# Gated recurrence and routed experts in one kernel: the turning of each unit's outputs put behind its logits in six units, the matmuls of ones ahead of the work changed from 10 of 512 columns to 40 of 256, and the first unit's state products given another bank

## The chip, the core and the metric

One core of a Trainium2 chip runs the whole program. The metric is the time of one execution on the device in microseconds (us). Of the kernel before there are five timed executions and one that was profiled. Engine names are those of the profile: PE (matmul) and PEld (weight load) are TensorE, DVE is VectorE, ACT is ScalarE, POOL is GpSimd, SP is the engine whose queue issues most DMAs.

## What is computed

```python
# 4 batches x 8 heads, 768 steps, head dim 48
f = 1.0 / (1.0 + np.exp(-f_logit))
for t in range(S):
    state = f[:, :, t, :, None] * state + np.einsum('bhd,bhe->bhde', k[:, :, t], v[:, :, t])
    y[:, :, t] = np.einsum('bhd,bhde->bhe', q[:, :, t], state)
x = y.transpose(0, 2, 1, 3).reshape(3072, 384)
# 4 groups x 4 experts: argmax group, then argmax expert in it, weight g_w * e_w
h = np.maximum(xg[mask_e] @ w1[g, e], 0.0)      # 384 -> 1024
out[tok_idx] = combined[:, None] * (h @ w2[g, e])   # 1024 -> 384
```

## The kernel before, in words

**First stage: the recurrence, in units.** The 768 steps are cut into 6 pieces of 128 (`NC`), the 4 batches into 2 pairs; `units` (L561) lists the 12 units (piece c, pair s), unit i being `(i // 2, i % 2)`. A unit passes through stages, each a Python generator that yields between its parts: `c` (`bounded`, DVE cuts the gate logits off), `g` (`gated`, ACT Exp and Ln, then two running sums over time as matmuls with a triangle, tile cs, L616, and their exponentials, L617 and L618), `m` (`multiplied`, DVE, L636 and L639), `t` (`turned`, 16 transposes of q and k on PE, L650, with four ACT copies, L651), `s` (`scored`, q times k on PE, tile ap, and a mask by DVE, tile am; units 3 to 8 in a halved form, L689 and L692, the others whole, L704 and L707), `n` (`stated`, the products of k and v for the next state, tile ds, L721, and DVE's update of the state, L726 to L729), `w` (`weighed`, the outputs, tile y: the state's part L741, the masks' part L745 or L753; ACT copies them to xT, L756), `d` (`done`, logits lT, L769, an ACT copy L771, and their transposition lg, L774), `x` (`listed`: 8 transposes of the outputs to rows, tile x_ps, L794, and three ACT copies, L796 and L799; these rows are what the experts gather later), `z` (`crossed`, ACT copies, L667), `b` (`decayed`, a transposition of the pieces' decays, tile gt, L659, for which a small DMA, ends, L623, must have landed).

**Order.** PE, DVE, ACT and SP take their instructions in the order in which the program issues them (`manual_schedule`, L85). That order is written out as lists of tokens: `BEGIN` (L844) for the first units, then one list for each i from 3 to 12: `ODD` or `EVEN` (L848, L849), or an entry of `ORDERS`. A token `x-1` in the list of i means: the next part of stage x of unit i-1. `r` advances the routing of a finished piece (`route`, L188): DVE one-hots, a few bf16 matmuls for ranks (tile rk, L213 and L215) and for a table (tile tb, L261, which takes DVE's val, L243), and DMAs of weights and tokens by POOL (L256). `l` issues the loads of a later unit on SP (L591), `o` (L807) writes kept rows to DRAM from SP, `k` (L817) loads the second weights of two early experts, `e` advances these experts.

**PSUM.** Seven banks go round under one tag (`bank`, L80); the eighth belongs to the state products alone: tile ds, allocated once, L534. So every unit's products go to the same place, and the next unit's must wait until DVE has read the last ones.

**Before the first unit** PE multiplies ones with ones (L892 to L894): 10 bf16 matmuls of 512 columns, whose result nobody reads. They wait for nothing but DVE's fill of the ones (L107).

**Second stage: the experts.** Rows are gathered by POOL (xg, L404), turned (L440, or by DVE, L426), multiplied with w1 (hp, L450), rectified by ACT (L451), multiplied with w2 (yo, L471 and L486), scaled, and scattered by POOL (L461). Weights of 1.5 MB each stream in on SP.

Of the kernel before, what the change touches and what calls it, by code (L numbers as in the profile page):

```python
# [10 lines left out]
FP32 = mybir.dt.float32  # L11
# [7 lines left out]
P = 128  # L19
# [4 lines left out]
def kernel(  # L24
# [12 lines left out]
    nc = tc.nc  # L37
    B, H, S, D = q.shape
# [7 lines left out]
    HP = H // 2  # L46
    DP = 64
# [29 lines left out]
    def const(shape, dtype, name):  # L77
        return cp.tile(shape, dtype, tag=name, name=name)

    def bank(shape, name):  # L80
        return ps.tile(shape, FP32, tag="bank", name=name)
# [11 lines left out]
    onesb = const([P, P], BF16, "onesb")  # L93
# [305 lines left out]
    def fetch(pool, rows, n, top=N, late=False):  # L399

        w = {"n": n, "pool": pool, "early": top < N, "late": late, "blocks": [(j, min(P, n - j * P)) for j in range((n + P - 1) // P)]}
        w["x"] = pool.tile([P, len(w["blocks"]), RW], FP32, tag="xg", bufs=2 if pool is ep else 6, name="xg")
        for j, m in w["blocks"]:
            nc.gpsimd.indirect_dma_start(out=w["x"][:, j, :], out_offset=None, in_=x_dram[0:1 + top, :], in_offset=bass.IndirectOffsetOnAxis(ap=rows[:, j:j + 1], axis=0))  # L404
        return w
# [124 lines left out]
    with ExitStack() as fast:  # L530
        sb = fast.enter_context(tc.tile_pool(name="sb", bufs=2))
        fp = fast.enter_context(tc.tile_pool(name="fp", bufs=1))
        sums = fast.enter_context(tc.tile_pool(name="sums", bufs=1, space=bass.MemoryType.PSUM))
        ds = sums.tile([P, 2, HP, D], FP32, tag="ds", name="ds")  # L534

        def kept(shape, name):
            return fp.tile(shape, FP32, tag=name, name=name)
# [24 lines left out]
        NU = len(units)  # L562
# [21 lines left out]
        def load(i, names):  # L584
            c, s = units[i]
            w = live.setdefault(i, {"v": pads["v"][i % 4], "qh": pads["qh"][i % 3]})
            for nm in names:
                if nm not in w:
                    w[nm] = sb.tile([P, 2, H, D], FP32, tag="ld_" + nm, bufs=3 if nm == "f" else 2, name="ld_" + nm)
                for b in parts(i) if nm == "f" else (slice(0, 2),):  # L590
                    nc.sync.dma_start(out=heads(w[nm][:, b])[:, :, 0:D], in_=SRC[nm][2 * s + b.start:2 * s + b.stop, :, c * P:(c + 1) * P, :].rearrange("b h t d -> t (b h) d"))  # L591
# [118 lines left out]
        def stated(i):  # L710

            c, s = units[i]
            w = live[i]
            if c == NC - 1:
                return
            old, new = states[s][c % 2], states[s][(c + 1) % 2]
            wide = D if i else DP
            for a in range(HP):
                for b in range(2):
                    for r in range(2):  # L720
                        nc.tensor.matmul(ds[DP * r:DP * r + wide, b, a, :], lhsT=w["kh"][:, b, 2 * a + r, 0:wide], rhs=w["v"][:, b, 2 * a + r, 0:D], start=True, stop=True)  # L721
            yield
            dst = new[:, :, :, 0:D]
            gv = w["g"].unsqueeze(3).broadcast_to((P, 2, HP, D))
            if c:
                nc.vector.tensor_tensor(dst, old[:, :, :, 0:D], ds, OP.add)  # L726
                nc.vector.tensor_tensor(dst, dst, gv, OP.mult)
            else:
                nc.vector.tensor_tensor(dst, ds, gv, OP.mult)  # L729
            yield  # L730
# [103 lines left out]
        def advance(gens):  # L834
# [6 lines left out]


        STAGES = {"c": bounded, "g": gated, "m": multiplied, "t": turned, "z": crossed, "s": scored, "n": stated, "w": weighed, "d": done, "x": listed, "b": decayed}
        BEGIN = """c0 g0 p g0 g0 m0 m0 m0 m0 l2 t0 t0 t0 t0 h c1 g1 g1 s0 s0 s0 s0 g1 g1 p w0 w0 n0 m1 m1 m1 m1 l3 h x0 x0 x0  # L844
            t1 t1 t1 t1 b1 c2 g2 g2 s1 s1 s1 s1 p d0 g2 g2 n0 n1 w1 w1 m2 m2 l4 n1
            d0 x1 x1 t2 t2 t2 t2 c3 g3 g3 x1 s2 s2 s2 s2 w2 g3 g3 d1 w2 n2 m3 m3 c4 g4 g4""".split()
        BEGUN = 3
        EVEN = "l+2 d-2 n-1 r r r x-1 x-1 t t t t g+1 g+1 x-1 r z s s w s s c+2 d-1 g+2 w g+2 n m+1 m+1".split()  # L848
        ODD = "l+2 d-2 r r x-1 x-1 t t t t b n-1 g+1 g+1 x-1 r z s s w s s c+2 d-1 g+2 w g+2 n m+1 m+1 r n".split()  # L849
        ORDERS = {  # L850
            NU - 4: "l+2 o d-2 n-1 r r r x-1 x-1 t t t t g+1 g+1 x-1 r z s s w s s c+2 d-1 g+2 w g+2 n m+1 m+1".split(),
            NU - 3: "l+2 o d-2 r r x-1 x-1 t t t t b n-1 r g+1 g+1 x-1 r s s s s c+2 w d-1 g+2 w g+2 n m+1 m+1 r n".split(),
            NU - 2: "d-2 r x-1 x-1 r t t t t r g+1 g+1 x-1 s s s s w d-1 w n m+1 m+1 k".split(),
            NU - 1: "d-2 r r n-1 x-1 x-1 t t t t r x-1 r s s s s w b d-1 w r r".split(),
            NU: "d-2 r e d-1 x-1 x-1 d-1 x-1 r r r e e r e r r e r r e r e r r e e e e e".split(),
        }
# [2 lines left out]
        def step(nm, i):  # L859
            if nm == "r":  # L860
                advance(routes)
            elif nm == "e":
                next(first[0], None)
            elif nm == "p":
                next(pad)
            elif nm == "o":
                send_kept(i - (NU - 4))
            elif nm == "k":
                load_second()
            elif nm == "h":  # L870
                next(turning)
            elif 0 <= i < NU:
                if nm == "l":

                    load(i, ("k", "qh"))
                    if i + 1 < NU:
                        load(i + 1, ("f",))
                    load(i, ("v",))
                    return
                if (nm, i) not in steps_of:  # L880
                    steps_of[nm, i] = STAGES[nm](i)
                next(steps_of[nm, i], None)
# [6 lines left out]
        load(1, ("qh", "k"))  # L889
        load(2, ("f",))  # L890
        load(1, ("v",))
        warm = bank([P, 4, P], "warm")  # L892
        for _ in range(10):
            nc.tensor.matmul(warm, lhsT=onesb, rhs=onesb.unsqueeze(1).broadcast_to((P, 4, P)), start=True, stop=True)  # L894
        for tok in BEGIN:
            step(tok[0], int(tok[1:] or 0))
        for i in range(BEGUN, NU + 1):
            if i == BEGUN:
                nc.sync.dma_start(out=x_dram[0:1, 0:DM].rearrange("o (h d) -> o h d", d=D), in_=blank[:, 0:D].unsqueeze(1).broadcast_to((1, H, D)))
                nc.sync.dma_start(out=x_dram[0:1, DM:RW], in_=blank[:, D:D + 2])  # L900
            for tok in ORDERS.get(i, ODD if i % 2 else EVEN):
                step(tok[0], i + int(tok[1:] or 0))
# [62 lines left out]
    for n in range(GE - 1):  # L965
        w = ws[n]
# [105 lines left out]
    with tc.If(more > 0), ExitStack() as late:  # L1072
# [5 lines left out]
        with tc.For_i(0, last, 1) as i:  # L1078
# [14 lines left out]
            w = fetch(ep, row, P, late=True)  # L1093
# [32 lines left out]
```

## Time and profile before

| | |
|---|---|
| median of 5 executions | 420.17 us (418.87 to 421.61) |
| the profiled execution | 421.64 us; its span, first to last instruction, 419.8 us |
| PE, PEld | 97%, 89% of the span |
| DVE, ACT, POOL | 63%, 39%, 20% |
| recurrence, about 0 to 135 us | PE has 4143 matmuls in all, some 2500 of them here |
| granted TensorE clock, mean | 0.99 |

The span is the time between the first and the last instruction; 1.84 us of the execution lie around it. In a row of the timeline stand the start, the length, the engine, the source line, the tile written and read, and the count of instructions merged into the row; brackets hold the engine's idle time before it and what ended it. A float32 matmul of the program shows as two records. PE rows are pipelined: a record's length is longer than the distance to the next record's start, so costs on PE are read from start to start.

### The profile page before, as it was taken

The numbers are of one execution on the slowest core, as the hardware profiler recorded it, in microseconds if no ns is written. First come the engines' busy times: TensorE is split into PE (matmuls) and PEld (weight loads), VectorE is DVE, ScalarE is ACT, GpSimd is POOL, SyncE is SP. The second block draws the span as 40 slices with busy tenths as digits, with TensorE's granted clock in tenths as the row PEclk, the third lists the DMA queues.
The fourth block names the chain that finished last, engine by engine and source line by source line (L and its number), as shares of the span: only waits on it lengthen the run. The fifth ranks groups of instructions, "written<-read, shape, count | busy, mean of one in ns | idle before, by whom it ended". The sixth has DMA issues, their size and how long they took to land.

```text
span 419.8 us, 10271 instructions
## 1 busy us (share of the span) xinstructions
PE 406.4 (97%) x4143; PEld 373.1 (89%) x4143; DVE 264.2 (63%) x780; ACT 162.5 (39%) x365; POOL 84.5 (20%) x132
## 2 busy tenths in 40 slices
PE   8989999998999998999999999999999999999994
PEld 3878878887878967979999999999999999999992
DVE  6666777877987801450699786495595595594230
ACT  6767878887555201111223122231231231231220
POOL 5000010101022075001031321311222231120230
PEclk9999999999999998799999999999999999999999
DMA  9999987879999189937539386595595695595010
GB/s 184 209 215 196 191 161 145 165 159 261 266 361 366 53 295 336 346 106 267 193 138 314 112 303 214 191 326 170 207 323 189 223 317 186 212 319 161 28 47 24
DMA packets 132146, 88.99 MB, mean 212 GB/s; under 512 B 102582, under 2 KB 122748, under 8 KB 132090
## 3 DMA queue, kind: packets, MB, share of 16 engines
q1 hardware_dynamic: 125666, 75.50, 60.8%
q0 software_dynamic: 5792, 11.92, 9.4%
q10 hardware_dynamic: 632, 0.83, 0.6%
q8 instruction: 35, 0.57, 0.5%
q14 instruction: 21, 0.17, 0.1%
HBM read 78.71 MB, written 9.83 MB: 211 GB/s over the span
## 4 chain that ended last, share of the span: by engine, by line
PE 46%; issue 30%; DMA 9%; DVE 6%; POOL 6%; POOLq 1%; ACT 0%; SPq 0%; DVEq 0%
PE hp L450 13%; PE yo L486 6%; DMA out_dram<-yt,xg 6%; PE yo L471 4%; POOL out_dram L461 4%; PE cs L616 3%; POOL xg L404 2%; PE y L745 2%; PE ap L704 2%; PE x_ps L794 2%; PE tr_k L650 2%; PE tr_q L650 2%; PE ap L689 2%; PE y L741 2%; PE y L753 2%
## 5 line engine op out<-in xcount | busy, mean ns | idle before, releaser
L450 PE MATMUL hp<-xe,w 128*128 128x128 f32 (+14 forms) x864 | 142.9, 325 | 1.9 <-issue 1.9
L450 PEld LDWEIGHTS hp<-xe,w 128*128 128x128 f32 x864 | 138.6, 193 | 4.3 <-issue 2.8
L486 PE MATMUL yo<-h,w 128*128 128x230 f32 (+13 forms) x672 | 115.8, 333 | 0.0
L433 DVE STREAM_TRANSPOSE yr<-yT 32x192 f32<-32x192 f32 (+1 forms) x208 | 70.5, 339 | 70.5 <-ACT yT L487 67.9
L486 PEld LDWEIGHTS yo<-h,w 128*128 128x128 f32 x672 | 113.7, 190 | 0.2
L451 ACT ACTIVATE h<-hp 128x256 f32<-128x256 f32 (+14 forms) x72 | 34.3, 478 | 110.0 <-PE hp L450 101.0
L426 DVE STREAM_TRANSPOSE xe<-xg 32x192 f32<-32x192 f32 (+1 forms) x208 | 69.7, 335 | 9.5 <-PE hp L450 6.5
L461 POOL DMA_INDIRECT out_dram<-yt,xg x32 | 34.6, 1080 | 156.9 <-ACT yt L458 151.3
L487 ACT COPY yT<-yo 128x230 f32<-128x230 f32 (+13 forms) x42 | 13.5, 325 | 80.5 <-PE yo L486 80.5
L404 POOL DMA_INDIRECT xg<-x_dram,rows_p x30 | 29.7, 990 | 51.1 <-DMA out_dram<-yt,xg 25.1
L471 PE MATMUL yo<-w,h 128*128 128x384 f32 x64 | 21.3, 486 | 0.0
L707 DVE TENSOR_TENSOR am<-ap,tri 128x512 f32<-128x512 f32 x24 | 14.9, 681 | 7.4 <-PE ap L704 7.4
L616 PE MATMUL cs<-ld_f,tri 128*128 128x384 f32 x48 | 18.6, 506 | 0.1
L471 PEld LDWEIGHTS yo<-w,h 128*128 128x128 f32 x64 | 11.9, 190 | 7.4
L458 ACT ACTIVATE yt<-yr,xg 128x384 f32<-128x384 f32 (+13 forms) x26 | 14.4, 604 | 5.4 <-DVE yr L433 5.4
L623 POOL DMA_DIRECT2D ends<-eq x10 | 5.4, 543 | 53.7 <-ACT eq L617 53.7
L756 ACT COPY xT<-y 128x512 f32<-128x512 f32 x24 | 13.4, 587 | 6.5 <-PE y L745 5.4
L692 DVE TENSOR_TENSOR am<-ap,seen 128x384 f32<-128x384 f32 x24 | 12.2, 552 | 5.4 <-PE ap L689 5.4
L651 ACT COPY Tq<-tr_q 128x512 f32<-128x512 f32 x24 | 15.0, 625 | 0.4 <-PE tr_q L650 0.3
L651 ACT COPY Tk<-tr_k 128x512 f32<-128x512 f32 x24 | 15.1, 635 | 0.0
L650 PE MATMUL tr_q<-ident,qh 128*128 128x128 f32 x96 | 14.5, 273 | 0.5 <-issue 0.3
L441 DVE COPY xe<-xg_ps 128x384 f32<-128x384 f32 (+1 forms) x4 | 2.1, 535 | 20.6 <-remote 9.7
(187 smaller groups left out, 446.4 us busy)
## 6 DMA issues: line engine op xcount, KB each, us to landing
w<-in_moe_w_dram SPq DMA_DIRECT2D x34, 1536.0 KB, 7.3
qh<-in_q_dram SPq DMA_DIRECT2D x12, 384.0 KB, 6.8
ld_k<-in_k_dram SPq DMA_DIRECT2D x12, 384.0 KB, 4.0
v<-in_v_dram SPq DMA_DIRECT2D x12, 384.0 KB, 5.7
ld_f<-in_f_logit_dram SPq DMA_DIRECT2D x11, 384.0 KB, 5.4
x_dram<-x_kept SPq DMA_DIRECT2D x2, 1536.0 KB
x_dram<-x POOLq DMA_DIRECT2D x2, 384.0 KB
x_dram<-x ACTq DMA_DIRECT2D x2, 384.0 KB, 6.2
```

What stands on the lines that cost most here:

```text
L404: nc.gpsimd.indirect_dma_start(out=w["x"][:, j, :], out_offset=None, in_=x_dram[0:1 + top, :], in_offset=bass.IndirectOffsetOnAxis(ap=rows ...
L426: squares(w, lambda n, k_, rk, g, rg: nc.vector.transpose(out=xT[rg, 0:n, k_], in_=x[rk, 0:n, g]))
L433: squares(w, lambda n, k_, rk, g, rg: nc.vector.transpose(out=y[rk, 0:n, g], in_=yT[rg, 0:n, k_]))
L450: nc.tensor.matmul(hp[:, o, :], lhsT=w1[:, ko, (f + o) * P:(f + o + 1) * P], rhs=w["xT"][:, ko, :], start=(ko == 0), stop=(ko == KO - 1))
L451: nc.scalar.activation(h[:, f:f + 2, :], hp, AF.Relu)
L461: sent = nc.gpsimd.indirect_dma_start(out=out, out_offset=bass.IndirectOffsetOnAxis(ap=w["x"][0:m, j, DM + 1:RW].bitcast(U32), axis=0), in ...
L471: nc.tensor.matmul(yp, lhsT=w["h"][:, fo, :], rhs=w2[:, fo, :], start=(fo == 0), stop=(fo == FO - 1))
L486: nc.tensor.matmul(yp, lhsT=w2[:, fo, m * P:(m + 1) * P], rhs=w["h"][:, fo, :], start=(fo == 0), stop=(fo == FO - 1))
L616: nc.tensor.matmul(cs.rearrange("t h d -> t (h d)"), lhsT=tri, rhs=nl[:, b], start=True, stop=True)
L650: nc.tensor.transpose(out=pt[:, a, :], in_=w[nm + "h"][:, b, 2 * a:2 * a + 2, :].rearrange("t r d -> t (r d)"), identity=ident)
L651: nc.scalar.copy(w["T" + nm][:, b], pt)
L707: nc.vector.tensor_tensor(am[:, r], ap[r], tri.unsqueeze(1).broadcast_to((P, HP, P)), OP.mult)
```

## The change

Three places change.

1. In the lists for i = 3 to 8 (`EVEN`, `ODD` and the entry for NU - 4 = 8) the three parts of `x-1` leave their places ahead of and behind `t`, and stand together behind `d-1`; `d-1` itself moves from behind `c+2` (DVE) to ahead of it. In the list for i = 10 (NU - 2) the third `r` moves from ahead of `g+1 g+1` to behind them.
2. The matmuls of ones: 40 of 256 columns in place of 10 of 512.
3. `stated`: unit 0's products go to a bank of the round, units 1 to 10 to the tile of their own, there called `later`; unit 1's products are written 64 wide, as unit 0's, not 48.

```diff
-        ds = sums.tile([P, 2, HP, D], FP32, tag="ds", name="ds")
+        later = sums.tile([P, 2, HP, D], FP32, tag="ds", name="ds")
...
-            wide = D if i else DP
+            wide = D if i > 1 else DP
+            ds = later if i else bank([P, 2, HP, D], "ds")
...
-        EVEN = "l+2 d-2 n-1 r r r x-1 x-1 t t t t g+1 g+1 x-1 r z s s w s s c+2 d-1 g+2 w g+2 n m+1 m+1".split()
-        ODD = "l+2 d-2 r r x-1 x-1 t t t t b n-1 g+1 g+1 x-1 r z s s w s s c+2 d-1 g+2 w g+2 n m+1 m+1 r n".split()
+        EVEN = "l+2 d-2 n-1 r r r t t t t g+1 g+1 r z s s w s s d-1 x-1 x-1 x-1 c+2 g+2 w g+2 n m+1 m+1".split()
+        ODD = "l+2 d-2 r r t t t t b n-1 g+1 g+1 r z s s w s s d-1 x-1 x-1 x-1 c+2 g+2 w g+2 n m+1 m+1 r n".split()
         ORDERS = {
-            NU - 4: "l+2 o d-2 n-1 r r r x-1 x-1 t t t t g+1 g+1 x-1 r z s s w s s c+2 d-1 g+2 w g+2 n m+1 m+1".split(),
+            NU - 4: "l+2 o d-2 n-1 r r r t t t t g+1 g+1 r z s s w s s d-1 x-1 x-1 x-1 c+2 g+2 w g+2 n m+1 m+1".split(),
             NU - 3: "l+2 o d-2 r r x-1 x-1 t t t t b n-1 r g+1 g+1 x-1 r s s s s c+2 w d-1 g+2 w g+2 n m+1 m+1 r n".split(),
-            NU - 2: "d-2 r x-1 x-1 r t t t t r g+1 g+1 x-1 s s s s w d-1 w n m+1 m+1 k".split(),
+            NU - 2: "d-2 r x-1 x-1 r t t t t g+1 g+1 r x-1 s s s s w d-1 w n m+1 m+1 k".split(),
...
-        warm = bank([P, 4, P], "warm")
-        for _ in range(10):
-            nc.tensor.matmul(warm, lhsT=onesb, rhs=onesb.unsqueeze(1).broadcast_to((P, 4, P)), start=True, stop=True)
+        warm = bank([P, 2, P], "warm")
+        for _ in range(40):
+            nc.tensor.matmul(warm, lhsT=onesb, rhs=onesb.unsqueeze(1).broadcast_to((P, 2, P)), start=True, stop=True)
```

## The prediction, made before the result was known

> **What bounds the kernel now.** I read the page first, then PE's waits in the recurrence, then the timeline where the change acts. On the page:
>
> ```profile
> PE 406.4 (97%) x4143; PEld 373.1 (89%) x4143; DVE 264.2 (63%) x780; ACT 162.5 (39%) x365; POOL 84.5 (20%) x132
> PE   8989999998999998999999999999999999999994
> PEclk9999999999999998799999999999999999999999
> ```
>
> PE is busy in every slice, so a change pays only where PE idles, or where its instructions get cheaper; and a delay of PE is not made up later. Idle time is short: PE's waits between 5 and 140 us (total, times, longest) are almost all of it.
>
> ```profile
> PE ds L721 <- DVE st L729: 1.2, 1, 1.2
> PE gt L659 <- DMA ends<-eq: 0.9, 1, 0.9
> PE tb L261 <- DVE val L243: 0.9, 1, 0.9
> PE y L753 <- issue: 0.8, 1, 0.8
> ```
>
> The change touches the first and the third of these. It also adds work ahead of the first unit and moves the turning of outputs. I sum in the time of PE, against the profiled execution (421.64 us: span 419.8 and 1.84 around it).
>
> **Part 1: the matmuls of ones.** The start, from the timeline:
>
> ```profile
> 1.05 4.37 PE L894 MATMUL warm<-onesb 128*128 128x512 bf16 x10 [1.05 <-DVE onesb L107]
> 4.87 0.52 ACT L610 ACTIVATE ld_f<-ld_f 128x384 f32<-128x384 f32 x1
> 5.49 1.83 PE L616 MATMUL cs<-ld_f,tri 128*128 128x384 f32 x4
> 8.50 0.65 PE L650 MATMUL tr_q<-ident,qh 128*128 128x128 f32 x4 [0.24 <-DVE qh L636]
> ```
>
> Ten matmuls of 512 columns end at 5.42, and the gates that the first sums need are ready at 5.39: the ones cover a wait, and hardly more. They go at some 0.427 us each, so 256 columns cost 0.213 at that speed. At what speed is that? Later, the same form of L450 passes in a stretch where half the clock was granted and in one where all of it was (windows of L450 alone; count of PE records in brackets, granted clock behind the PEld column):
>
> ```profile
> 167.30:172.30 5.00, 5.00 (x14) 4.45 (x14) 0.50 1.05 388
> 173.00:178.00 5.00, 5.00 (x27) 4.90 (x26) 1.00 0.82 319
> ```
>
> 14 records against 27 in 5 us: a factor of 1.93, so 256 columns cost about 0.11 us at full clock. The four records of the first sums take 1.83 from 5.49, with the second pair's gates ready only at 6.36; later sums take 1.56, and at half clock they would take about twice that. So I place the rise of the clock at about 5.4. Bounds: all 40 at full clock end at 1.05 + 40 x 0.11 = 5.45 (no delay); all 40 at half clock end at 1.05 + 40 x 0.213 = 9.6 (4.1 us of delay). I take the place seen: 4.35 / 0.213 = 20 at half clock, 20 at 0.11 = 2.2, end at 7.6. The first sum starts 2.1 us late. What depends on it: both sums then follow each other (1.56 for four records in the row at 12.95, so done at 9.1, against 7.32), second eq at 9.13, qh 0.5 later and 0.57 long, so the transposes of 8.50 start at about 10.2: **+1.7 us**, not 2.1, because the second sum no longer waits for its own gates. From 8.50 to 24.2 PE runs without a gap, so the delay stays. The loads do not absorb it: the second unit's gates have landed by 9.9 and their sums run only at 12.95.
>
> [...]
>
> **Part 2: the first products.** At the second unit:
>
> ```profile
> 22.67 1.56 PE L616 MATMUL cs<-ld_f,tri 128*128 128x384 f32 x4
> 24.83 0.55 DVE L729 TENSOR_TENSOR st<-ds,decays 128x384 f32<-128x384 f32 x1
> 25.43 0.92 PE L721 MATMUL ds<-v,kh 128*48 128x48 f32 x32 [1.20 <-DVE st L729]
> ```
>
> Unit 1's products wait until DVE has read unit 0's from the same bank. With a bank of its own that wait of 1.2 goes. Next late would be am (masked scores) for the outputs behind: done at 23.8, with the delay 25.5; the outputs start after that. Unit 1's products become 64 wide: the 64-wide form at 16.24 takes 1.02 to the next group, the 48-wide one here 0.75, so +0.25. Together -0.95. Order on SP, POOL and DVE is not changed by it. Unit 0's bank is taken out of the round from 16.2 until DVE's update; the next user of it is unit 2's first transposition, whose q comes after that update on DVE anyway, so it adds no wait. If it did, at most the 1.2 would come back.
>
> **Part 3: outputs turned behind the logits, six units.** One unit now, PE and DVE:
>
> ```profile
> 66.97 0.64 PE L769 MATMUL lT<-xT,gw 128*32 128x128 f32 x16
> 68.03 0.39 PE L753 MATMUL y<-am,v 128*48 128x64 f32 x3
> 68.16 0.26 PE L753 MATMUL y<-am,other 128*48 128x64 f32 x1
> 70.35 1.04 PE L794 MATMUL x_ps<-ident,xT 128*128 128x128 f32 x8
> ```
>
> ```profile
> 67.08 1.02 DVE L692 TENSOR_TENSOR am<-ap,seen 128x384 f32<-128x384 f32 x2 [0.52 <-PE ap L689]
> ```
>
> The second half of the outputs resumes at 68.16, just after DVE's second mask at 68.10: a stall too short to be listed. With 0.87 of turning ahead (70.35 to 71.22) the mask is long there. Gain: the outputs' rows step 0.055 per pair; between 68.08 and 68.16, and in the refill behind it, some 0.1 is lost per unit. Loss: the turning now stands between matmuls of other tile shapes. A transposition follows another after 0.11, but a change of shape costs 0.20 (62.30 to 62.83 is 0.53 for four, against 0.44 within): 0.09 per unit. **Net 0 to -0.1 in six units.** ACT's three copies move with it: they used to stand ahead of the copies L651, now they stand between the logits' copy (67.68) and Exp L607 (68.60, before which ACT idles 0.66, and 0.89 before the logits' copy). They take 0.8 of ACT; Exp slips by about 0.5, Ln L610 from 71.25 to some 72.0, and the sums that need it start at 73.0: 0.9 of cover left. L651 starts with 71.9 now and 72.0 then. Banks: the turning takes those of the masked scores, free by 67.6. The rows are written to DRAM (token o) two lists later, so no DMA waits for them. Nothing is queued behind on POOL; SP's order is the same. Bounds: -0.85 x 6 below (if all the turning time hid in stalls, which PE's waits exclude), +0.8 x 6 above (if all of ACT's 0.8 reached PE).
>
> **Part 4: the third r in the list of i = 10.** PE waits 0.86 at 116.72 for DVE's val, then does the sums in 1.47 to the next group. Sums first: they start at 115.7 (gates ready at 114.2), the table's matmuls follow at 117.2, when val (116.7) is done. Gain 0.86, and about 0.05 of it less by shape. DVE's order stays: table update at 117.9 as before, then the early rows at 119.3, then the masks, which are 0.2 earlier and now the next late: the outputs would start at 121.0 and need the last mask at 121.9, when it is done. So **-0.85**, with 0 as the bound above.
>
> **Sum:** +1.7 - 0.95 - 0.05 - 0.85 = -0.15; bounds by the ones alone: -1.85 (no delay) to +2.2 (all 40 at half clock). 421.64 - 0.15 = 421.5 for an execution like the profiled one, which was 1.47 over the median of the five; from the median, **420.0 us**. A measurement of this kernel tells about 0.5% (2.1 us) from no change, so I forecast no difference that counts.
>
> **Rivals.**
> *The stall of the experts goes.* From 162.4 to 166.1 PE crawls though it waits for nothing the page names, and then runs at half clock for 6.8 us: some 3 us of stall and 3.4 of half speed. Nothing in the change aims at it, but PE's stream shifts by 60 instructions and its time by parts of a us. For: no data dependence ends it. Against: five executions within 2.8 us of each other suggest that it recurs. Half of it gone: 416.8; all gone: 413.6. Chance 0.17.
> *The small stalls at 58.3 (0.85) and 104.8 (0.94) go as well*, by the same shift, with a clock that rises early: 420.0 - 1.8 - 0.8 = 417.4. Chance 0.10.
> *ScalarE becomes late (slower).* Place: the six units; ACT's copies of turned rows stand ahead of Exp and Ln of the unit after next. It decides as soon as Ln slips over 0.9 us; I count 0.75. Each 0.1 beyond costs 0.6 in six units; if the slip is 1.5, 3.6 us: 423.6. For: ACT is busy 16.5 of each 20 us in 60 to 100. Against: its two idle gaps in a unit, 1.5 us, are just where the copies go. Chance 0.12.
> *The ones stay at half clock to their end*: 420.0 + 2.2 = 422.2 (or worse with a stall placed badly). Chance 0.13, a bit over half of it beyond 0.5%.
> *It does not do what it says* (the products wait elsewhere, val is late again): 420.0 + 0.95 + 0.85 = 421.8, inside the forecast's zone.
>
> **Numbers.** Forecast zone 0.48 with its own range 418.2 to 422.2. Faster 0.28 (the first two rivals and a bit), slower 0.20 (the third, and half of the fourth), the rest within 0.5%: 0.52. The range leaves out the whole stall gone and the far end of a late ScalarE: 415.8 to 423.2.
>
> **What would show it.** Right: L616's first row at 7.5 to 7.7 and the transposes of 8.50 at 10.2; no wait of ds on st; L753 in one run without a break, and the unit's period still 10.1 to 10.2; no wait of tb on val. Wrong: L616 later than 8.5 (clock), idle PE ahead of cs in units 4 to 9 (ScalarE), a period under 9.9 (shapes cheaper than I count), or a PE row at 160 to 175 that has no crawl.

## The result, and the profile after

The changed kernel takes 420.10 us (median of 44 executions, 418.18 to 422.63); the kernel before, measured beside it, 420.79 us (86 executions). The ratio is 0.9981, with a 95% interval of 0.9970 to 0.9992: some 0.8 us sooner, within the 0.5% that was called no change. The profiled execution of the changed kernel took 418.73 us, its span 416.9: 2.9 us less than that of before. The two profiles must be taken apart before that is credited to the change.

Times in us at which the same group of PE starts in the two profiles:

| | before | after | difference |
|---|---|---|---|
| first cs | 5.49 | 7.02 | +1.53 |
| second unit's cs | 12.95 | 14.23 | +1.28 |
| fourth unit's cs | 33.96 | 34.17 | +0.21 |
| lT of unit 8 | 109.58 | 108.06 | -1.52 |
| lT of unit 9 | 121.33 | 119.29 | -2.04 |
| first hp of the experts | 135.50 | 134.24 | -1.26 |
| fourth group of hp | 157.61 | 156.35 | -1.26 |
| third group of yo | 179.20 | 176.45 | -2.75 |
| last PE instruction ends | 414.26 | 411.51 | -2.75 |

From the third group of yo to PE's last instruction all fourteen profiles of this document take 235.06 us, on both chips, and from the first to the fourth group of hp 22.11 (21.89 where a run says "late e"). So two things set a profile's time almost alone: when the first hp comes, and how long the stretch between the fourth hp and the third yo takes.

PE's waits between 5 and 140 us after the change (total, times, longest); the lines of ds, gt and y are gone, tb has come three times in other places, and xg_ps is new:

```profile
PE tb L261 <- DVE val L243: 0.8, 3, 0.3
PE xg_ps L440 <- DMA xg<-x_dram,rows_e: 0.7, 1, 0.7
PE tr_q L650 <- issue: 0.6, 1, 0.6
```

The start, in the timeline:

```profile
1.05 6.14 PE L895 MATMUL warm<-onesb 128*128 128x256 bf16 x40 [1.05 <-DVE onesb L107]
7.02 1.46 PE L616 MATMUL cs<-ld_f,tri 128*128 128x384 f32 x4
9.05 1.37 PE L650 MATMUL tr_q<-ident,qh 128*128 128x128 f32 x8 [0.58 <-issue]
```

The forty ones give way at 7.0, the first sums now all run at full clock, which was granted from 4.36 on, and in one piece (1.46 instead of 1.83), and the first eight transposes run together from 9.05, where before four started at 7.63 and four at 8.50. One of the six units, again PE in the timeline, to set against the rows from 66.97 to 70.35 of before:

```profile
65.51 0.64 PE L770 MATMUL lT<-xT,gw 128*32 128x128 f32 x16
66.08 1.09 PE L795 MATMUL x_ps<-ident,xT 128*128 128x128 f32 x8
67.10 0.32 PE L754 MATMUL y<-am,v 128*48 128x64 f32 x4
...
68.73 0.93 PE L722 MATMUL ds<-v,kh 128*48 128x48 f32 x32
```

From start to start the outputs (L754) take 1.63 and have no break (1.79 before); the turned rows cost 1.02 in place of 0.87. The one pays for the other. But further on in the lists of even i, a wait is new. DVE and PE in the timeline, before and then after:

```profile
73.89 0.49 DVE L243 TENSOR_TENSOR val<-head,part 128x128 bf16<-128x128 f32 x2
...
74.44 0.29 PE L261 MATMUL tb<-val,ln 128*128 128x64 bf16 x4
```

```profile
72.65 0.49 DVE L243 TENSOR_TENSOR val<-head,part 128x128 bf16<-128x128 f32 x2
...
73.21 0.29 PE L261 MATMUL tb<-val,ln 128*128 128x64 bf16 x4 [0.26 <-DVE val L243]
```

Before, PE came to tb at 74.44, when val (73.89 + 0.49 = 74.38) had just been made: the turned rows, standing ahead of the transposes, covered it. With them gone from there, PE is 0.26 early.

One thing changed that nobody edited. POOL's instructions in the timeline, before and then after:

```profile
96.60 0.79 POOL L256 DMA_DIRECT2D x_dram<-meta  x1 [10.10 <-DVE table L266]
97.38 0.52 POOL L623 DMA_DIRECT2D ends<-eq  x1
```

```profile
94.55 0.52 POOL L623 DMA_DIRECT2D ends<-eq  x1 [9.50 <-ACT eq L617]
...
95.57 0.79 POOL L256 DMA_DIRECT2D x_dram<-meta  x1 [0.31 <-POOL meta L255]
```

POOL is not among the engines of the hand-written order (L85): its order is the scheduler's, and it follows from the lists. Before, unit 9's ends stood behind the meta data of the routing, which wait for DVE; after, it goes ahead. That is the DMA that gt waited 0.94 for at 104.8. The order alone does not make that wait: the run with 20 ones (below) has the old order and issues the same DMA at the same 97.38, and gt does not wait there; in the profile of before the DMA also landed late, 7.29 us after its issue (4.05 in that of after). (The expectation of the six lists alone, below, calls it unit 7's, by mistake.)

### The profile page after: what moved, and what is told of

Read it like the earlier page. It is cut to its first block, busy times and chain, and to the rows that moved or that the text cites. A ratio compares the mean times of both kernels' runs of the same rounds, so it can differ in the third digit from the quotient of the medians.

```text
span 416.9 us, 10333 instructions
## 1 busy us (share of the span) xinstructions
PE 405.9 (97%) x4173; PEld 374.2 (90%) x4173; DVE 263.8 (63%) x780; ACT 162.6 (39%) x365; POOL 84.2 (20%) x132
## 4 chain that ended last, share of the span: by engine, by line
PE 46%; issue 30%; DMA 9%; DVE 7%; POOL 6%; POOLq 1%; ACT 1%; DVEq 0%
PE hp L450 13%; PE yo L486 6%; DMA out_dram<-yt,xg 6%; PE yo L471 4%; POOL out_dram L461 4%; PE cs L616 2%; PE x_ps L795 2%; POOL xg L404 2%; PE y L754 2%; PE ap L689 2%; PE ds L722 2%; DMA xg<-x_dram,rows_e 2%; PE tr_k L650 1%; PE warm L895 1%; PE y L742 1%
## 5 line engine op out<-in xcount | busy, mean ns | idle before, releaser
L450 PE MATMUL hp<-xe,w 128*128 128x128 f32 (+14 forms) x864 | 141.2, 322 | 2.2 <-issue 2.2
L450 PEld LDWEIGHTS hp<-xe,w 128*128 128x128 f32 x864 | 137.2, 192 | 4.2 <-issue 2.5
```

Source lines behind the costliest of these rows:

```text
L450: nc.tensor.matmul(hp[:, o, :], lhsT=w1[:, ko, (f + o) * P:(f + o + 1) * P], rhs=w["xT"][:, ko, :], start=(ko == 0), stop=(ko == KO - 1))
```

## The experiments

All ratios are to the kernel before on the same chip. A ratio is not the quotient of the two medians; for the moved r below that quotient would be 0.9983, its ratio is 1.0000. Eight kernels ran on one chip (kernel before: 420.79 us beside the four parts alone, 420.62 us beside the last four runs), four on another (415.13 us); the last section says what differs there. The fourth unit's cs (33.96 before) serves as a mark from which the stretch behind it is measured without the start.

**Each part alone.** First the ones (`range(40)`, 256 wide), nothing else.

```diff
-        warm = bank([P, 4, P], "warm")
-        for _ in range(10):
+        warm = bank([P, 2, P], "warm")
+        for _ in range(40):
```

> Only the ones are changed (40 of 256 columns), the rest is the kernel before. Theory: the delay is PE time at the very start and nothing absorbs it. The ones go at about 0.15 us each over both speeds of the clock (150 ns mean step in the profile of the changed kernel), so the first sum starts at 7.0 to 7.6 us in place of 5.49, the transposes of 8.50 at 9.8 to 10.2, and the first hp of the experts (135.50) at 136.8 to 137.2: +1.3 to +1.7 us, ratio 1.003 to 1.004. Rival: a later wait for a DMA (ends at 104.8, the early gather ahead of 132.8) swallows it: the first hp within 0.4 us of 135.5, ratio 1.000 to 1.001.

Measured: 421.31 us, ratio 1.0022 (1.0004 to 1.0040). First sum at 8.09, second unit's sum at 15.30, first hp at 136.85. The clock rose later in this execution (6.54 us, against 4.36 in the changed kernel's profile). The rival falls by the first hp, which is 1.35 later than before's and not within 0.4; the interval leaves out 1.000, though not 1.001, the rival's upper end.

The bank alone:

```diff
-            wide = D if i else DP
+            wide = D if i > 1 else DP
+            ds = later if i else bank([P, 2, HP, D], "ds")
```

> Only the first products' bank is changed. Theory: the wait of 1.20 us of ds on st goes, the products cost 0.21 to 0.25 more because they are 64 wide, so the third sum after it (cs at 33.96) starts 1.0 us sooner, and the first hp too: 134.5, ratio 0.9975. Rival: the gain is given back at a wait whose end another engine sets (ends at 104.8, or the early gather, which the profile of the changed kernel shows as 0.71 us of PE waiting for xg): first hp at 135.1 or later, ratio 0.999 or more.

Measured: 419.72 us, ratio 0.9973 (0.9948 to 0.9998). From the third unit's cs to the fourth's it is 10.23 us, 11.29 before: 1.06 less. First hp at 134.87, with a wait of 0.54 for the gather. The median carries the whole 1.1 us, the profile only 0.6 of it at the first hp; both readings lie in the interval.

The six lists alone (EVEN, ODD and NU - 4 as in the diff of the change):

```diff
-        EVEN = "l+2 d-2 n-1 r r r x-1 x-1 t t t t g+1 g+1 x-1 r z s s w s s c+2 d-1 g+2 w g+2 n m+1 m+1".split()
+        EVEN = "l+2 d-2 n-1 r r r t t t t g+1 g+1 r z s s w s s d-1 x-1 x-1 x-1 c+2 g+2 w g+2 n m+1 m+1".split()
```

> Only the six units' lists are changed. Theory: the move itself comes out even on PE (1.02 for the turned rows instead of 0.87, 1.63 for the masks' outputs instead of 1.79), it opens a wait of 0.22 to 0.26 us for val in each of units 5, 7 and 9, and it changes the order on POOL's queue, where ends of unit 7 now goes ahead of the rows' meta data that wait for DVE's table; so the wait of 0.94 us for ends at 104.8 goes. Sum at the logits of unit 8 (109.58): +0.66 - 1.0 = -0.3 us, and about as much at the first hp; ratio 0.999 to 1.000. Rival (the recorded prediction): no such wait appears and none goes, -0.05 us; then val does not show as a wait and gt still waits 0.9 us for ends.

Measured: 420.46 us, ratio 0.9999 (0.9979 to 1.0019). PE's waits:

```profile
PE tb L261 <- DVE val L243: 1.6, 4, 0.9
PE ds L721 <- DVE st L729: 1.2, 1, 1.2
PE xg_ps L440 <- DMA xg<-x_dram,rows_e: 0.7, 1, 0.7
```

Three of the four waits of tb are the new ones (0.25 each), the fourth is that of i = 10; the wait of gt is gone, and POOL's order is the new one, so it is this part that moves it. Lists of an even and an odd i together (cs of unit 6 to cs of unit 8) take 20.51, against 20.30 before: three times +0.21 is +0.6 us. Both figures return wherever nothing else stalls: 20.51 in six profiles with the lists turned, 20.3 in five without. The ratio shows no such loss; more on this below.

The moved r alone:

```diff
-            NU - 2: "d-2 r x-1 x-1 r t t t t r g+1 g+1 x-1 s s s s w d-1 w n m+1 m+1 k".split(),
+            NU - 2: "d-2 r x-1 x-1 r t t t t g+1 g+1 r x-1 s s s s w d-1 w n m+1 m+1 k".split(),
```

> Only the third r of the list of i = 10 is moved. Theory: the wait of 0.86 us for val goes on PE, but the early gather is not sooner, since it waits for the meta data that DVE writes after val, and DVE is not sooner; PE had about 0.4 us to spare at xg_ps (132.83). So the logits of unit 9 (121.33) come 0.5 to 0.8 sooner, xg_ps waits 0.2 to 0.5 for the gather, the first hp is 0.2 to 0.5 sooner; ratio 0.999. Rival (the recorded prediction): the first hp is 0.85 us sooner, 134.65, with no wait of xg_ps; ratio 0.998.

Measured: 420.06 us, ratio 1.0000 (0.9980 to 1.0020). POOL in the timeline of before, then POOL and PE in that of this run:

```profile
118.55 0.76 POOL L256 DMA_DIRECT2D x_dram<-meta  x1 [2.37 <-DVE number L304]
125.09 1.08 POOL L404 DMA_INDIRECT xg<-x_dram,rows_e  x1 [5.78 <-DVE dl L199]
```

```profile
117.65 0.76 POOL L256 DMA_DIRECT2D x_dram<-meta  x1 [2.36 <-DVE number L304]
126.77 1.06 POOL L404 DMA_INDIRECT xg<-x_dram,rows_e  x1 [8.36 <-DVE run L224]
```

```profile
133.56 0.52 PE L440 MATMUL xg_ps<-ident,xg 128*128 128x128 f32 x3 [1.48 <-DMA xg<-x_dram,rows_e]
```

The wait for val is gone and PE reaches unit 10's logits (128.19) 2.0 us sooner than in the profile of before. Of that, 1.1 lies between unit 9's turned rows and its logits, where the r stands; the rest is mostly stalls of the profile of before that this one lacks. Then PE stands 1.48 us at xg_ps, and the first hp (136.10) is 0.6 later than before's, not the 0.2 to 0.5 sooner that was expected. The gather may only start when the meta data, issued after val, are in DRAM: 9.1 us here from issue to gather, 6.5 to 7.7 us in the other profiles. In all fourteen the gather starts 0.86 us after the last completion that the trace has of this write, and the write of the rows themselves is complete before it. (The name in the bracket, DVE run, had nothing to do with it: it is dl in the profile of before, boost in that of after, pick and best in others, while the 0.86 us is the same.)

**Parts taken back from the changed kernel** (on the second chip). The old ones:

```diff
-        warm = bank([P, 2, P], "warm")
-        for _ in range(40):
+        warm = bank([P, 4, P], "warm")
+        for _ in range(10):
```

> The changed kernel with the ten 512-column matmuls of ones of the kernel before; its other edits stay. Theory: the ones' delay moves all engines alike, the early gather too, so it comes back whole: first sum at 5.4 to 5.5 us in place of 7.02, first hp 1.3 to 2.0 us sooner than the changed kernel's usual place, ratio to the kernel before 0.994 to 0.996. Rival: the gather's landing, not PE, sets the experts' start and does not move with the ones: xg_ps then waits 2 us in place of 0.71 and the ratio stays at 0.998.

Measured: 413.19 us, ratio 0.9960 (0.9946 to 0.9974). First sum at 5.53; xg_ps waits 0.58, not 2: the gather moves with the start, and the theory holds.

The old list for i = 10:

```diff
-            NU - 2: "d-2 r x-1 x-1 r t t t t g+1 g+1 r x-1 s s s s w d-1 w n m+1 m+1 k".split(),
+            NU - 2: "d-2 r x-1 x-1 r t t t t r g+1 g+1 x-1 s s s s w d-1 w n m+1 m+1 k".split(),
```

> The changed kernel with the list of i = 10 of the kernel before (third r ahead of the gates' sums). Theory: the moved r saves PE a wait (0.86 us) that the early gather takes back, since DVE's val and the meta data the gather waits for are no sooner; so PE waits 0.85 us for val again, xg_ps waits 0.9 less (about none), and the first hp stays within 0.2 us of where it is for the same length of the meta data's DMA; ratio to the kernel before 0.998. Rival (the recorded prediction): the 0.85 us come back on the end, ratio 1.000.

Measured: 414.86 us, ratio 0.9991 (0.9981 to 1.0002). The interval holds the rival's 1.000 and leaves out the 0.998 that was expected. Between this and the run above lie 1.67 us, of which the ones' start is 1.4 (below): some 0.2 is left for the r. But in the profiles the first hp lies 100.7 us after the fourth unit's cs here, and 99.9 to 100.1 in the three profiles with the moved r and the new lists (the run above, and the changed kernel twice). So the profiles allow the r 0.6 to 0.8 and the medians 0.2; with one profile of this form, and a meta write that varies by 2.6 us, the remainder is not settled.

**What the gather covers.** With the old ones, the first e of the list of i = 12 put behind a part of the last unit's logits and turned rows:

```diff
-            NU: "d-2 r e d-1 x-1 x-1 d-1 x-1 r r r e e r e r r e r r e r e r r e e e e e".split(),
+            NU: "d-2 r d-1 x-1 x-1 e d-1 x-1 r r r e e r e r r e r r e r e r r e e e e e".split(),
```

> As the changed kernel with the old ones, and in the list of i = 12 the first e (the turning of the first gathered rows, xg_ps) stands behind the first d-1 and two x-1, so that 1.4 to 1.6 us of PE work that does not need the gather (lT, x_ps) stand ahead of the wait. Theory: the gather's landing is the bound at that place, in most executions; the wait of 0.7 to 1.5 us is filled, the first hp is 0.7 to 1.0 us sooner than with the old ones alone, ratio to the kernel before 0.991 to 0.994. Rival: the work put ahead is only moved, and the turned rows become late for the first hp: the same time as with the old ones alone, 0.994 to 0.996.

Measured: 412.49 us, ratio 0.9938 (0.9923 to 0.9952). No wait of xg_ps is listed. The median is 0.7 better than without the edit, though the two intervals still touch; in the profile the third group of hp is 0.3 sooner, once a stall of 0.45 in unit 8's ds, which the other run lacks, is taken off. Of eleven profiles with the early e, ten wait for the gather (0.2 to 1.5); of three with the late e, none. The profile of before is the eleventh: two stalls, at 58.3 and 104.8, had made PE late there.

The same e, bank and r on the kernel before, without the turning and with the old ones:

> The kernel before with three edits: the first products' bank, the moved r of i = 10, and the first e behind d-1 x-1 x-1 in the list of i = 12. No turning behind the logits, old ones. Theory: the wait of ds (1.0 net) and the wait for val (0.85) both reach the end, because the gather has 1.5 us of cover more: 1.5 to 1.9 us, ratio 0.9955 to 0.9965. Against the run with turning and the old ones and the late e it tells what the turning is worth: by PE's rows it loses 0.7 us (three waits for val) and wins about 0.9 (the DMA of ends ahead of the meta data on POOL), so the two should be within 0.5 us. Rival: the gather still bounds: xg_ps waits, and the ratio is that of the bank alone, 0.9973.

Measured: 412.91 us, ratio 0.9947 (0.9931 to 0.9962), with no wait of xg_ps; the rival's 0.9973 lies outside. Both this and the run above beat the kernel before, and their ratios are below both of the changed kernel's (0.9981, and 0.9985 further down), though that one ran on the other chip. Between the two, turning or not, no difference can be told: the medians say 0.4 us for the turning, the profiles 0.5 against it.

**An error of mine.** The next kernel has bank, r and late e, and turns only in EVEN and NU - 4.

```diff
-        EVEN = "l+2 d-2 n-1 r r r x-1 x-1 t t t t g+1 g+1 x-1 r z s s w s s c+2 d-1 g+2 w g+2 n m+1 m+1".split()
+        EVEN = "l+2 d-2 n-1 r r r t t t t g+1 g+1 r z s s w s s d-1 x-1 x-1 x-1 c+2 g+2 w g+2 n m+1 m+1".split()
```

> The kernel before with the first products' bank, the moved r of i = 10, the late first e of i = 12, and the turning behind the logits only in the lists of even i (4, 6 and 8); the lists of odd i and the ones stay as before. Theory: in the odd lists the turned rows covered the wait for val, so with them back ahead of the transposes the three waits of 0.25 us do not appear, and the order on POOL stays the new one (ends ahead of the meta data): 0.5 to 0.75 us sooner than the run with all six units turned, the old ones and the late e; ratio to the kernel before 0.991 to 0.993. Rival: the waits for val only move to another place, ratio 0.994 as in that run.

Measured: 419.95 us, ratio 0.9979 (0.9963 to 0.9995).

```profile
PE tb L261 <- DVE val L243: 2.1, 3, 0.9
```

I had the lists the wrong way round: g+1 and the r behind it make unit i+1's sums, so the tb that comes behind the sums of units 5, 7 and 9 stands in the lists of even i, and those are the ones I left turned. The waits grew from 0.25 each to 0.89, 0.89 and 0.36. It refutes the expectation, and it supports the cause: what the wait depends on is the turned rows ahead of it in that list. The mirror image, with only the odd lists turned, was not run.

**The changed kernel again, and the number of ones**, on the first chip.

> The changed kernel once more, on the chip of the kernels beside it. Theory: first sum at 6.8 to 8.1 us according to where the clock rises, three waits of 0.25 us for val, no wait of ds or gt, a wait of 0.2 to 1 us of xg_ps for the gather; ratio to the kernel before 0.997 to 0.999, whatever the chip's own level. Rival: the gain of the first comparison came from a stall at 58.3 or 162 us that one chip has and another has not; then the ratio is 1.000.

Measured: 419.62 us, ratio 0.9985 (0.9966 to 1.0004). Three waits of 0.25 for val, xg_ps 0.54, first sum at 7.29, first hp at 134.44: much as in the first profile. The interval holds the expected 0.997 to 0.999 and the rival's 1.000 alike, so this run does not decide between them.

No ones at all:

```diff
-        for _ in range(10):
+        for _ in range(0):
```

> The kernel before without any matmul of ones. Theory: the clock rises only after a stretch of PE work, so the first sums (4 records) and the transposes behind them run at half clock: 2.9 us for the sums in place of 1.83, the second unit's first sum (12.95) about 1 us later, ratio 1.002 to 1.003; the ones are worth that and 40 of them cost more than they bring. Rival: PE waits there for loads and for DVE, so it costs nothing: second unit's first sum within 0.3 us of 12.95, ratio 1.000.

Measured: 422.05 us, ratio 1.0034 (1.0008 to 1.0060).

```profile
5.35 2.90 PE L616 MATMUL cs<-ld_f,tri 128*128 128x384 f32 x4 [5.35 <-POOL blank L177]
8.19 2.19 PE L650 MATMUL tr_q<-ident,qh 128*128 128x128 f32 x8
```

The sums take 2.90 where they take 1.46 at full clock, and the second unit's sum starts at 14.11, 1.2 later than before. The granted clock rose at 10.07, 4.72 us after PE's first work.

Twenty ones of 256 columns:

```diff
-        warm = bank([P, 4, P], "warm")
-        for _ in range(10):
+        warm = bank([P, 2, P], "warm")
+        for _ in range(20):
```

> The kernel before with 20 matmuls of ones of 256 columns, as many columns as ten of 512. Theory: the time goes by columns and clock, so nothing changes: the last of the ones ends near 5.4 us, first sum at 5.36 to 5.53, ratio 1.000; the delay of the changed kernel is then the doubled number of columns alone. Rival: each instruction has a price of its own, 0.02 us or more, and the first sum starts 0.4 us or more later.

Measured: 420.40 us, ratio 0.9998 (0.9976 to 1.0020).

```profile
1.04 4.16 PE L894 MATMUL warm<-onesb 128*128 128x256 bf16 x20 [1.04 <-DVE onesb L107]
5.35 0.88 PE L616 MATMUL cs<-ld_f,tri 128*128 128x384 f32 x2
```

As many columns in twice the instructions take no longer, 4.16 us (4.37 before); the first sum starts at 5.35 (5.49), the second unit's at 12.96 (12.95). The cost of the change's ones is the doubled number of columns.

## Why the prediction was right, and where it was not

The time was right. Of the four parts, the ones and the first products came out nearly as counted, the six units did not, and what the third r brings at the end is not settled.

| term | predicted | measured on PE | how |
|---|---|---|---|
| ones | +1.7 | +1.4 | second unit's sum: mean 14.52 in four profiles with 40, 13.08 in nine with as many columns as before |
| first products | -0.95 | -1.06 | third to fourth unit's sum, bank alone |
| six units | -0.05 | +0.6 where nothing else stalls | 20.51 against 20.30 for two lists, three times |
| third r | -0.85 | -1.1 on PE, 0 to -0.8 at the end | unit 9's turned rows to its logits: 7.16 against 8.27; then the gather |

On PE alone the measured terms sum to -0.1, where -0.15 was predicted: the six units are off by +0.65, the other three together by about as much the other way. That this cancels is luck. So is the nearness of 420.0 to the measured 420.1: the forecast stood on a median of five executions, 420.17, and 86 of the same kernel give 420.79. At the end of the kernel, where the r brings 0 to -0.8, the terms sum to +0.2 to +1.0, and measured is -0.8 (-1.3 to -0.3). The ratios of the four parts alone, with up to 1 us of uncertainty on each, add to -0.25 us and contradict neither.

**Part 1.** The prices were right: from start to start the ones take 0.213 up to the rise at 4.36, which makes 15.5 of the 40, and 0.109 after it; the other 24.5 end at 7.03, and the first sum starts at 7.02. What was mis-sized is the place of the rise. I put it at 5.4; the profiles with ones have it from 4.0 to 7.0 (that of before at 5.20), that is 2.97 to 5.99 us after PE's first work. The first sum follows it: 6.85 with the rise at 4.01, 8.09 at 6.54, about half a us for each us. The rival in which the ones stay at half clock to their end did not occur in a profile. Its price was too high: where 0.4 of a delay is absorbed, as in the forecast, 4.1 becomes 3.7, and the upper bound +1.85, not +2.2.

From one profile to the next the rise comes up to 3.0 us earlier or later after PE's first work (2.97 to 5.99 us; 4.72 us with no ones at all). What sets it, no run shows. The 0.8 that the second rival adds for an early rise was an estimate; the earliest one, at 4.01, brought the first sum at 6.85, 0.75 ahead of the 7.6 foreseen.

**Part 2** held, and the worry about the bank taken out of the round did not come true: no wait of unit 2's transposes.

**Part 3** failed in two sentences. "Net 0 to -0.1 in six units" counted the move itself, and that part is right (1.63 and 1.02, sum 2.65; 1.79 and 0.87 before, sum 2.66). It did not ask what had stood behind the old place: tb, covered by those 0.87 of turned rows. I had gone through the waits that exist, not through the ones that 0.87 less of PE work would open. And "Nothing is queued behind on POOL" took POOL's order for granted, although only four engines have a written one. The wait for ends was in two of seven profiles with the old order and in none of seven with the new; in the pair of profiles its disappearance looks like a gain of 0.94. It isn't quite: in the profiles without it, some 0.5 to 0.6 comes back at unit 9's outputs (2.4 to 2.5 from start to start in most, in place of 1.92). ScalarE's rival did not occur: Exp slips 0.5 as counted, Ln ends 0.85 ahead of the sums that need it (70.65 and 71.50; before, 71.25 and 72.97), the 0.9 of cover that was counted, and no sum waits.

**Part 4.** "So -0.85, with 0 as the bound above": the runs lie between the two (ratio 1.0000 alone, with 0.8 us to either side; 0.2 us by the medians and 0.6 to 0.8 by the profiles in the changed kernel). What the working lacked is the gather. I followed DVE's masks as next late, and stopped at unit 10. The next late thing is the gather, which hangs on val and not on PE, and takes back some or all of the gain; before's profile hid it, because PE was late there for other reasons.

**The rest of the 2.9 us between the two profiles.** 1.0 is the stall at 58.3, which comes and goes (present in the profile with 20 ones, absent in that of the six lists). 1.5 is the stall of the experts, the first rival: half clock lasted 6.83 us in the profile of before and 3.41 in that of after. But it did not go by the change. The mean granted clock is on record for each execution, and in the profiles 0.990 goes with 6.83 us and 0.992 to 0.994 with 3.41. Of the kernel before, 17 of 70 executions beside the eight kernels of the first chip have 0.991 or less; of the changed kernel, 12 of 58. The second rival, the small stalls at 58.3 and 104.8 going, did come about between the two profiles, but it too belongs to the pair: other profiles of the old lists lack one or both.

**What the terms leave out.** From the fourth unit's cs to the logits of unit 8 the seven profiles with the old lists take 73.7 to 75.8 us, 74.6 on average; the six with all six lists turned take 73.9 to 74.3, 74.0 on average. So the turned lists, which cost 0.6 where nothing else stalls, are 0.6 shorter on average. The difference is stalls. Each of the seven has at least one at y or ds that the profile ends by "issue", that is, by no wait it can name; they come to some 0.5 to 2.9 us a profile, and two of the seven have the wait for ends besides. Four of the six have none, the other two 0.2 and 0.45. Such a gain of about 1.2 would bring the terms to what was measured. It is a count of thirteen profiles and no run tests it: the six lists alone gave 0.9999.

## What to carry to other kernels

When work is moved away from ahead of an instruction, list what it was covering there, for every list and for every engine whose order nobody wrote down, as carefully as what it will meet in its new place. Before a saving on the busiest engine is credited, follow the next DMA that it will wait for back to what issues it: a gain ahead of a gather that hangs on another engine stops at the gather (of 1.1 us on PE, 0 to 0.8 came through here), until independent work is put in front of the wait (none of the three profiles with the late e waits for the gather). Matmuls of ones ahead of the work pay here up to the moment the first data land (none at all cost 1.4 us), and columns beyond it are a delay (twice the columns cost 1.4 us).

## What the runs showed of the hardware

**The stall of the experts goes with the chip.** From the fourth group of hp to the third of yo it is 21.6 us in the profile of before, 20.1 and 20.4 in the two of the changed kernel, and 15.3 in all four of the second chip, with the same instructions there. Windows of the changed kernel, then of its run with the old ones on the second chip (length; busy time and count of PE, PEld, DVE, ACT and POOL; granted clock, DMA share, GB/s):

```profile
160.00:170.00 10.00, 7.83 (x38) 6.61 (x37) 4.95 (x14) 1.39 (x4) 2.58 (x3) 0.83 1.03 367
```

```profile
160.00:170.00 10.00, 10.00 (x57) 9.81 (x56) 5.51 (x16) 2.19 (x5) 1.46 (x2) 1.00 1.03 385
```

On the second chip PE has no gap there and the clock stays whole, while the DMA engines are as busy. The other ten profiles take 19.9 to 21.6 us; that is about the 5.6 us between the two chips' times for the kernel before. What makes PE crawl on the one and not on the other stays open.

**The half clock has a fixed place.** In all ten profiles with the stall the clock falls 160.43 us after its rise, 47 times 3.413, be the rise at 4.31 or at 10.07 (from 5.20 to 165.62 in the profile of before, from 4.36 to 164.78 in that of after; granted clock 0.50 behind the fall); it stays down for 3.413 us (seven) or 6.827 us (three), that is, once or twice the same length. The four profiles without the stall have no such fall. PE was idle in the 3.413 us ahead of the fall for pieces of at most 1.3 us, 1.3 to 2.6 us in all (1.62 in the profile of before, 1.81 in that of after). What makes the clock fall there, no run shows. Which of the two lengths comes changes from execution to execution: those with a mean clock of 0.991 or less take 1.2 to 1.4 us longer in the median than the others, in either kernel, and that much of the 4 us of spread of one kernel is this, not the change.

**A small write is slow among big loads.** The meta data's DMA (8 bytes a row, 512 rows), issued by POOL at 116 to 120 us while 1.5 MB weights stream in (DMA share 1.0), was complete 5.6 to 8.3 us later, and the gather went 6.5 to 9.1 us after its issue. The same write for the last rows, at 139 to 145 us with a DMA share of 0.09 to 0.13, was complete after 2.2 to 2.3 us. The spread of the first moves the start of the experts by as much as the parts of this change are worth.

**Stalls without a name come with instruction loads.** Between 12 and 135 us the fourteen profiles have fourteen stalls of PE of 0.2 us or more that end by "issue". Twelve of them end 2.2 to 2.6 us after a packet of 16 KB starts on the trace's instruction queue q8, and they come back at the same places of PE's stream: at its matmul records 978 to 980 in four profiles, 1739 and 1740 in two, 1992 to 1995 in three. So they look like instructions that came late. No run here moves these loads, so the cause is not shown, nor why the turned lists have fewer of them.
